# Two attentions side by side: the projections of the first one move into the loop of the second

## The chip, the cores and the metric

The kernel runs on one core of a Trainium2 chip. The metric is the device time of one execution in microseconds; the median of three runs before the change is 1738.47 us.

Names used below: PE is the matrix engine (TensorE), PEld its weight loads, DVE VectorE, ACT ScalarE, POOL GpSimd, SP the engine that issues most DMAs. PSUM has eight banks of 128 x 512 fp32 here, tile `ps_st`, numbered 0 to 7.

## The reference

Two attention blocks over 2048 positions and 640 features, 32 heads of 20 features each, with inputs of their own; the result is `[a, b]` along the features. Block A looks back over a dilated window, block B is full attention:

```python
qkv = (x @ wqkv).reshape(B, S, 3, H, Dh)          # both blocks, S = 2048, H = 32, Dh = 20
# A: 8 keys per query, at distances 0, 2, ... 14; keys before position 0 are masked
idx = pos[:, None] - (arange(8) * 2)[None, :]
logits = einsum("bhsd,bhswd->bhsw", q, kg) * Dh ** -0.5
a = einsum("bhsw,bhswd->bhsd", softmax(where(mask, logits, -1e9)), vg) @ wo
# B: all keys
p = softmax(einsum("bhqd,bhkd->bhqk", q, k) * Dh ** -0.5)
b = einsum("bhqk,bhkd->bhqd", p, v) @ wo
```

## The kernel before

Every projection is done in split precision: each operand is a rounded "hi" and the rest "lo", and three products hi·hi, hi·lo, lo·hi (`PASSES`) are summed. With five chunks of 128 features (`KC = 5`) one result tile takes 15 matmuls. ACT makes hi by a copy that rounds, DVE or POOL make lo by a subtraction.

**Ahead of the loop.** In this order: A's q and k (three sets of columns, 512, 256 and 512 wide, over 16 tiles of 128 rows), B's q and k (10 column blocks by 4 row blocks, 40 groups of 15 full matmuls with 512 columns), then the v of A and of B in blocks (`v_group`), between which PE computes score maxima for the first `LEAD = 52` steps. q, k, v go to DRAM and come back in the layout that the attention wants (`b_pieces`). A's attention runs on POOL, with help from DVE and ACT (`a_attention`), and begins while B's q and k are projected (`a_pace`).

**The loop** goes over B's attention. A unit is four heads (`g`) by 512 queries (`qc`), 32 units; a unit has 16 key blocks of 128; so there are `NS = 512` steps, a unit's key block each. A step needs

- four score halves: each is one matmul with 62 weight rows (three times 20 for the split, 2 for the maxima) and 512 columns, and one exp on ACT into an `e` tile. Two heads lie in the upper and two in the lower 64 rows of PE, so two halves run side by side;
- four maxima halves (60 rows) for the unit to come, each reduced by DVE from PSUM, singly or two banks at once;
- one value product: four matmuls of 32 output rows each, by heads (`b_pv`).

The order in which these pieces stand is written out in a string, `ORDER`, for the first 488 steps; the last `TAIL = 24` steps are regular. Its tokens: `Y` one score half and one maxima half side by side, `S` two score halves, `M` two maxima halves with one reduce over two banks, `N` two with two reduces, `V` a value product and the end of a step (here the product of two steps earlier, `LAG = 2`), `H` three of the 15 pairs of a group of A's output projection, `j` a small transpose. The digits are PSUM banks. PE executes exactly this order, as do ACT and DVE their own parts: each engine's queue is strictly in program order.

In `b_pv` two key blocks are summed in a bank. ACT copies the sum to SBUF (`more`), POOL adds it to the unit's sum (`braw`), eight times in a unit less one. At a unit's end the sums of exps are inverted by way of DRAM (`normalize`) and POOL multiplies.

POOL's share in each step is set by `begin(i)`: pieces of A's attention are issued as long as POOL's estimated time stays within `AHEAD` of `i * STEP`, `STEP = 2.36` us. A finished tile of A is transposed by DVE and DMA (`a_turn`, `turn_parts`), and projected by `H` tokens (`out_chunk`): two matmuls of 64 rows and 320 columns side by side, into two banks, whose two results ACT copies out and POOL adds.

B's output projection starts when a block of 512 queries has all its heads. The blocks are worked off with full 320-column groups between the last steps (`fill`), and the last block after the loop.

All engine instructions are recorded by one helper, so every row of the profile names line 71; rows are told apart by tiles and shapes.

Of the kernel before, what the change touches and what calls it, by code (L numbers as in the profile page):

```python
# [16 lines left out]
D = 640  # L17
# [12 lines left out]
PAD = WIN - 1  # L30
PASSES = ((0, 0), (0, 1), (1, 0))


# [6 lines left out]
PB = 6  # L40
NQC = 4
NKB = 16
NS = NG * NQC * NKB
LEAD = 52
TAIL = 24
R_AHEAD = 3
LAG = 2
NEG = -1.0e30
STEP = 2.36
AHEAD = 2.4  # L50
QK_US = 3.42
V_US = 2.72
A_SLOW = 0.91
A_FROM = 1
# [3 lines left out]

# [17 lines left out]
def attention_pair(ctx, tc, xa, wqk_a, wv_a, wo_a, xb, wqk_b, wv_b, wo_b, oa, ob):  # L76
    nc = tc.nc
    PS = bass.MemoryType.PSUM
    const = ctx.enter_context(tc.tile_pool(name="const", bufs=1))
    sb = ctx.enter_context(tc.tile_pool(name="sb", bufs=1))  # L80
    ps = ctx.enter_context(tc.tile_pool(name="ps", bufs=1, space=PS))
# [10 lines left out]
    loop = [None, False]  # L92

    def odd(n):

        return n if loop[0] is None else n + (now[0] + n - loop[0] + 1) % 2

    soft_jobs, turn_jobs = [], []
    at_once = [True]
# [6 lines left out]
    def job(jobs, n, fn, *args):  # L106

        jobs.append((now[0] + n, fn, args))
        if at_once[0]:
            run_jobs(jobs, 1)  # L110

    def tick():
        now[0] += 1
        for fn, args in due.pop(now[0], ()):
            fn(*args)


    psb = ps.tile([128, 8, 512], F32, name="ps_st")
    free = list(range(4))
    pair = [0]  # L120
    taken = {}
    given = []

    def bank():

        n = given.pop(0) if given else free.pop(0)
        t = psb[:, n]
        taken[id(t)] = (None if loop[0] is not None and loop[1] else n, t)
        return t

    def give(t):

        n = taken.pop(id(t))[0]
        if n is not None:
            free.append(n)

    def wide():

        pair[0] += 1
        return psb[:, 4 + 2 * (pair[0] % 2):6 + 2 * (pair[0] % 2)]  # L140

    def all_banks():
        while True:
            w = [wide(), wide()]
            for n in range(4):
                yield w[n % 2][:, n // 2]
                t = bank()
                give(t)
                yield t

# [10 lines left out]
    wait = [1]  # L161

    def split(hi, lo, src, tag="stg", second=None, first=None):

        t = sb.tile([128, 640 if tag == "stg" else 1024], F32, tag=tag, bufs=3 if tag == "stg" else PB, name="stg")
        raw = t[:, :src.free_size()] if len(src.shape) == 2 else (
            t[:, :src.shape[1] * src.shape[2]].rearrange("p (k c) -> p k c", c=src.shape[2]))
        sp.dma_start(raw, src)

        def parts():  # L170
            (first or act.copy)(hi, raw)
            (second or dve).tensor_tensor(lo, raw, hi.bitcast(F32), ALU.subtract)
        after(odd(wait[0]), parts)

    PAIRS = ((0, 2), (2, 4), (4, 5))

    def columns(n):

        return (sb.tile([128, 2, KC - 1, 512], F32R, tag="big", bufs=4, name="xn"),
                sb.tile([128, 2, 1, 512], F32R, tag=f"last{n % 4 // 2}", bufs=2, name="xl"))  # L180

    def chunk(t, xi, k):
        return t[k // (KC - 1)][:, xi, k % (KC - 1)]

    def x_pieces(x, n, second=None):

        t = columns(n)
        src = x[:, n * 512:(n + 1) * 512].rearrange("(k p) c -> p k c", p=128)

        def piece(a, b):  # L190
            u = t[a // (KC - 1)]
            m = a % (KC - 1)
            split(u[:, 0, m:m + b - a], u[:, 1, m:m + b - a], src[:, a:b], "p", second)
        return t, [lambda a=a, b=b: piece(a, b) for a, b in PAIRS]

    def wide_pieces(src, second=None, first=None):

        w = [sb.tile([128, KC, 320], F32R, tag="w", bufs=4, name="ww") for _ in range(2)]
        return w, [lambda a=a, b=b: split(
            w[0][:, a:b], w[1][:, a:b], src[:, a:b], second=second, first=first or second and gp.tensor_copy) for a, b in PAIRS]  # L200


    WA = 512
    A_COLS = [0, 512, 768, 2 * D]
    NA = len(A_COLS) - 1
    AK = ((0, 3), (3, KC))

    def a_parts(w, to, raw, k0, k1):
        for half, (a, b) in enumerate(AK):
            a0, b0 = max(a, k0), min(b, k1)  # L210
            if a0 < b0:
                u = slice(a0 - a, b0 - a)
                act.copy(w[0][half][:, u, to], raw[:, a0 - k0:b0 - k0])
                dve.tensor_tensor(w[1][half][:, u, to], raw[:, a0 - k0:b0 - k0], w[0][half][:, u, to].bitcast(F32), ALU.subtract)

    def a_piece(w, to, src, k0, k1, tag="stg"):

        n = to.stop - to.start
        t = sb.tile([128, 640], F32, tag=tag, bufs=3 if tag == "stg" else 2, name="stg")
        if src.shape[1] == k1 - k0:  # L220
            raw = t[:, :(k1 - k0) * n].rearrange("p (k c) -> p k c", c=n)
            sp.dma_start(raw, src)
        else:
            raw = t[:, :n].unsqueeze(1)
            sp.dma_start(t[:, :512].rearrange("p (m c) -> p m c", c=128), src)
        after(wait[0], a_parts, w, to, raw, k0, k1)

    def a_weight():
        return [[sb.tile([128, 3, WA], F32R, tag="w", bufs=4, name="wc"),
                 sb.tile([128, 2, WA], F32R, tag="akv", bufs=4, name="wd")] for _ in range(2)]  # L230

    def a_pieces(g):
        w, out = a_weight(), []
        c0, end = A_COLS[g:g + 2]
        c = c0
        while c < end:
            n = min(128 - c % 128, end - c)
            out.append(lambda to=slice(c - c0, c - c0 + n), src=wqk_a[c // 128][:, :, c % 128:c % 128 + n]:
                       a_piece(w, to, src, 0, KC))
            c += n  # L240
        return w, out

    def m_pieces(m):
        w = sb.tile([128, 2, KC, 128], F32R, tag="w", bufs=4, name="w")
        return w, [lambda: split(w[:, 0], w[:, 1], wqk_b[m])]

    def rows15(p, o, W):

        for k in range(KC):
            for i, (wi, xi) in enumerate(PASSES):  # L250
                pe.matmul(p[:, :320], o(xi, k), W[wi][:, k], start=(k == 0 and i == 0), stop=(k == KC - 1 and i == 2))

    def a_rows(p, x, t, g, W, ks, passes=PASSES):
        n = A_COLS[g + 1] - A_COLS[g]
        for k in ks:
            for wi, xi in passes:
                pe.matmul(p[:, :n], chunk(x, xi, k)[:, t % 4 * 128:t % 4 * 128 + 128], W[wi][k // 3][:, k % 3, :n],
                          start=(k == 0 and (wi, xi) == PASSES[0]), stop=(k == KC - 1 and (wi, xi) == PASSES[-1]))

    def a_store(p, g, t):  # L260

        c0, end = A_COLS[g:g + 2]
        r = sb.tile([128, WA], F32, tag="ao", bufs=3, name="ro")
        act.copy(r[:, :end - c0], p[:, :end - c0])
        hf, r0 = divmod(t * 128, HS)
        c = c0
        while c < end:
            m, c1 = divmod(c, D)
            n = min(D - c1, end - c)
            dst, pad = ((qa_d, 0), (ka_d, PAD))[m]  # L270
            after(1, sp.dma_start, dst[hf, pad + r0:pad + r0 + 128, c1:c1 + n], r[:, c - c0:c - c0 + n])
            c += n

    def store_rows(p, dst):
        r = sb.tile([128, 320], F32, tag="r", bufs=4, name="ro")
        act.copy(r, p[:, :320])
        if id(p) in taken:
            give(p)
        after(1, sp.dma_start, dst, r)


    NT = S // 128
    banks = all_banks()


    W = a_weight()
    XA = [columns(0)]
    for k in range(KC):
        a_piece(W, slice(0, WA), wqk_a[:4, :, k].rearrange("m p c -> p m c"),
                k, k + 1, ("stg", "stg", "stg", "vb", "vb")[k])  # L290
        split(chunk(XA[0], 0, k), chunk(XA[0], 1, k), xa[k * 128:(k + 1) * 128, :512], "p")
    tick()
    t, more = x_pieces(xa, 1)
    XA.append(t)
    for fn in more:
        fn()
    tick()
    wait[0] = 3
    loads = []
    for n in (2, 3):  # L300
        t, more = x_pieces(xa, n)
        XA.append(t)
        loads += more
    ident = sb.tile([128, 128], F32, tag="aot", bufs=1, name="ident")
# [3 lines left out]
    warm = bank()  # L308
    for _ in range(19):
        pe.transpose(warm[:, :128], ident, ident)  # L310
    give(warm)

    mask = const.tile([128, WIN, H], F32, name="mask")
    gp.memset(mask, 0.0)
# [891 lines left out]
```

## Time and profile before

| quantity | value |
|---|---|
| runs | 1738.47 us median (1737.33 to 1738.79) |
| span of the profiled execution | 1736.3 us |
| first value product starts | 458.47 us |
| value product of step 480 starts | 1604.87 us |
| last value product starts | 1687.64 us |
| PE busy | 1724.5 us (99%) |
| DVE busy | 1348.7 us (78%) |
| ACT busy | 1338.9 us (77%) |
| POOL busy | 1266.2 us (73%) |

The busy time of an instruction runs from its start to its end. Instructions of one engine overlap at their edges, so the distance from one start to the next is shorter than the mean duration. In a row of a timeline stand the start, the length, the engine, the operation, output <- inputs and the count; in brackets what it waited for and how long.

### The profile page before, as it was taken

How to read it: one execution, taken by the hardware profiler on the slowest of the kernel's cores; microseconds unless marked ns; L12 is line 12 of the kernel's file. 1: busy time of each engine (PE TensorE's matmuls, PEld its weight loads, DVE VectorE, ACT ScalarE, POOL GpSimd, SP SyncE). 2: the span in 40 equal slices, each digit the busy share in tenths (PEclk: the TensorE clock that was granted, in tenths of full speed). 3: DMA queues.
4: the chain of work that ended last, by engine and by line, in shares of the span. 5: the costliest groups of instructions: out<-in, count | busy, mean ns of one | idle time of the engine just before them, and what ended most of it. 6: DMA issues, size and time to landing. Idle time of an engine off the chain costs nothing.

```text
span 1736.3 us, 34687 instructions
## 1 busy us (share of the span) xinstructions
PE 1724.5 (99%) x12711; PEld 1006.0 (58%) x12711; DVE 1348.7 (78%) x1825; ACT 1338.9 (77%) x2658; POOL 1266.2 (73%) x1122
## 2 busy tenths in 40 slices
PE   9999999999999999999999999999999999999999
PEld 8988889999545544444344444444444455434569
DVE  3113223988799999999999999999999999999300
ACT  4323224232699999999999999999999999999981
POOL 0000950999899999999999999999999963544242
PEclk9999999999999999999999999999999999999999
DMA  6347878866754365345436434542643532111123
GB/s 227 119 139 239 304 261 273 259 204 187 199 151 125 96 161 153 93 136 158 135 95 173 126 119 127 170 135 88 158 143 106 147 95 61 46 36 53 33 76 113
DMA packets 194436, 248.29 MB, mean 143 GB/s; under 512 B 89309, under 2 KB 114397, under 8 KB 193273
## 3 DMA queue, kind: packets, MB, share of 16 engines
q1 hardware_dynamic: 193688, 245.41, 47.1%
q8 instruction: 100, 1.64, 0.4%
q14 instruction: 72, 0.58, 0.1%
q10 hardware_dynamic: 576, 0.66, 0.1%
HBM read 181.08 MB, written 64.91 MB: 142 GB/s over the span
## 4 chain that ended last, share of the span: by engine, by line
PE 90%; POOL 4%; DVE 2%; ACT 1%; DMA 1%; issue 1%; SPq 0%; POOLq 0%; ACTq 0%; DVEq 0%
PE ps_st L71 90%; POOL akv L71 2%; DVE mx L71 1%; ACT e L71 1%; POOL xn L71 1%; DMA stg<-wv_b 0%; SPq L71 0%; POOL ww L71 0%; POOL xl L71 0%; POOL ao L71 0%; ACT more L71 0%; DMA vb_d<-ve 0%; POOL al L71 0%; DMA s_d<-sm 0%; DMA rb<-s_d 0%
## 5 line engine op out<-in xcount | busy, mean ns | idle before, releaser
L71 DVE TENSOR_REDUCE mx<-ps_st 128x1 f32<-128x512 f32 (+1 forms) x1504 | 1227.6, 875 | 57.3 <-PE ps_st L71 47.8
L71 ACT ACTIVATE e<-ps_st 128x512 f32<-128x512 f32 x2048 | 1066.7, 627 | 30.7 <-PE ps_st L71 16.8
L71 PE MATMUL ps_st<-bk,bq 60*128 60x512 f32 x2048 | 553.4, 436 | 1.0 <-ACT ve L71 0.5
L71 PE MATMUL ps_st<-bq,bk 62*128 62x512 f32 x2048 | 548.7, 433 | 5.6 <-ACT ve L71 3.0
L71 PE MATMUL ps_st<-e,vb 128*32 128x512 f32 x4096 | 543.0, 604 | 0.4
L71 PEld LDWEIGHTS ps_st<-bq,bk 62*128 62x128 f32 x2048 | 274.8, 184 | 403.3 <-ACT e L71 246.5
L71 POOL TENSOR_TENSOR braw<-braw,more 128x512 f32<-128x512 f32 x224 | 288.2, 1287 | 85.5 <-ACT more L71 85.1
L71 PEld LDWEIGHTS ps_st<-bk,bq 60*128 60x128 f32 x2048 | 257.1, 184 | 108.7 <-DVE mx L71 61.2
L71 POOL TENSOR_TENSOR akv<-akv,aq 128x1280 f32<-128x1280 f32 x64 | 188.9, 2951 | 166.4 <-DVE w L71 166.3
L71 POOL TENSOR_TENSOR akv<-akv 128x640 f32<-128x640 f32 (+3 forms) x304 | 282.2, 928 | 14.4
L71 ACT COPY ro<-ps_st 128x320 f32<-128x320 f32 (+2 forms) x172 | 73.7, 463 | 171.1 <-PE ps_st L71 122.7
L71 PE MATMUL ps_st<-ww,xn 64*128 64x320 f32 (+1 forms) x1776 | 187.1, 309 | 0.0
L71 PEld LDWEIGHTS ps_st<-ww,xn 64*128 64x128 f32 (+1 forms) x1776 | 175.7, 186 | 14.6 <-ACT e L71 8.3
L71 PEld LDWEIGHTS ps_st<-e,vb 128*32 128x32 f32 x4096 | 82.1, 108 | 149.0 <-issue 75.4
L71 POOL TENSOR_TENSOR akv<-akv,al 128x1280 f32<-128x1280 f32 x64 | 151.6, 2368 | 0.2
L71 ACT COPY more<-ps_st 128x512 f32<-128x512 f32 x224 | 136.3, 609 | 3.5 <-PE ps_st L71 1.5
L71 PE MATMUL ps_st<-xn,w 128*128 128x512 f32 x480 | 115.8, 390 | 0.0
L71 PEld LDWEIGHTS ps_st<-xn,w 128*128 128x128 f32 x480 | 90.1, 188 | 19.3
L71 ACT CAST pr<-ps_st 128x512 fp32r<-128x512 f32 x40 | 23.5, 587 | 98.8 <-PE ps_st L71 96.0
L71 PE MATMUL ps_st<-ww,aot 64*128 64x320 f32 x960 | 99.7, 308 | 0.0
L71 DVE TENSOR_TENSOR pr<-ps_st,pr 128x512 fp32r<-128x512 f32 x40 | 27.6, 691 | 86.7 <-ACT pr L71 86.7
L71 PEld LDWEIGHTS ps_st<-ww,aot 64*128 64x128 f32 x960 | 90.3, 186 | 5.8 <-POOL ao L71 0.6
(65 smaller groups left out, 1062.5 us busy)
## 6 DMA issues: line engine op xcount, KB each, us to landing
akv<-ka_d SPq DMA_DIRECT2D x128, 320.0 KB
akv<-va_d SPq DMA_DIRECT2D x128, 320.0 KB
kb_d<-pr SPq DMA_DIRECT2D x20, 512.0 KB
qb_d<-pr SPq DMA_DIRECT2D x20, 512.0 KB
bk<-kb_d SPq DMA_DIRECT2D x16, 640.0 KB
bq<-qb_d SPq DMA_DIRECT2D x64, 160.0 KB
stg<-xb SPq DMA_DIRECT2D x16, 512.0 KB
rb<-s_d SPq DMA_DIRECT2D x128, 64.0 KB
```

What stands on the lines that cost most here:

```text
L71: return self.tc.keep_in_program_order(op(*a, **k))
```

## The change

Only B's q, k and v are projected ahead of the loop: the 40 groups of q and k as before, then 16 groups of v with the maxima of 32 steps between.

A's q, k and v become 48 small groups in the loop (12 sets of 320 columns, the second six sets for the second half of the rows, four groups a set). A group makes two tiles of 128 x 320. It has 30 `F` tokens, each two matmuls of 64 rows and 320 columns side by side, one for each result, and holds its two banks throughout; rows are exchanged after 15, so that both halves of the features end up in the same bank. The 16 groups of A's output projection and 12 of B's take the same form (the halves are no longer added by POOL). 70 of the 76 groups are in the `ORDER`, six are left for the end.

The products of all 16 key blocks of a unit are summed in one bank; ACT copies it once, to the single tile `misc`. `V` now computes its own step's product. The `e` tiles are seven of 512 x 2 columns (in tiles called `big` and `last`). A's attention on POOL starts when its rows are there, about step 80, with `STEP = 2.8`. At the end the last unit's sums are broadcast by a matmul with a selection matrix and inverted by DVE.

```diff
-LEAD = 52
-TAIL = 24
-LAG = 2
-STEP = 2.36
+LEAD = 32
+NP = 7
+STEP = 2.8
...
-        if part == 0:
-            accs[u] = bank()
-        acc = accs[u]
-        for j in range(GH):
-            pe.matmul(acc[32 * j:32 * j + 32, :], stacks[g][2][:, kb, j * VC:j * VC + 32], P[i][j % 2][:, j // 2],
-                      start=(part == 0), stop=(part == 1))
...
-            more = spare[n % 2][:, n // 2 % 2]
-            act.copy(more, acc)
-            after(2, pool, raws[u], raws[u], more, ALU.add)
+        if kb == 0:
+            accs[u] = psb[:, ns[0]]
+            acc_n[0] = ns[0]
+        acc = accs[u]
+        for j in range(GH):
+            pe.matmul(acc[32 * j:32 * j + 32, :], vs[u // NQC][:, kb, j * VC:j * VC + 32], P[i][j % 2][:, j // 2],
+                      start=(kb == 0), stop=(kb == NKB - 1))
+        del P[i]
+        if kb == NKB - 1:
+            raw = misc[:, :512]
+            act.copy(raw, accs.pop(u))
+            if u < NU - 1:
+                normalize(raw, u, (lambda: out_last(u % NQC, raw)) if u // NQC == NG - 1 else None)
...
+    def f_tokens(lhs, rhs, n, ns):
+        for second in range(2):
+            for k in range(KC):
+                for i, (wi, xi) in enumerate(PASSES):
+                    for r in range(2):
+                        w = r ^ second
+                        rows = slice(r * HALF, r * HALF + HALF)
+                        pe.matmul(psb[:, ns[w], :n], lhs(w, xi, k)[rows], rhs(wi, k)[rows],
+                                  start=(second == 0 and k == 0 and i == 0), stop=(second == 1 and k == KC - 1 and i == 2))
+                    yield
...
+            parts(AW[si][0][:, :, c:c + n], AW[si][1][:, :, c:c + n], raw, second=gp if si < 6 else dve, end=1)
...
+    def a_group(si, n, a, ns):
+        if n % 2 == 0 and a == 0:
+            if si + 1 < NA:
+                spaced(set_pieces(si + 1, 3), 1, 2)
+        x, W = XA[n], AW[si]
+        yield from f_tokens(lambda w, xi, k: chunk(x, xi, k)[:, (2 * a + w) * 128:(2 * a + w + 1) * 128],
+                            lambda wi, k: W[wi][:, k], 320, ns)
+        for w in range(2):
+            store_rows(ns[w], dst[hf, pad + r0:pad + r0 + 128, si % 2 * 320:si % 2 * 320 + 320])
+            if si % 6 in (3, 5):
+                after(3, a_rows.__setitem__, si % 6 // 5, t + 1)
...
-        "Y07S61M2Y45V0Y71S26M3Y05V7Y06M3S52Y71V0Y26M3S75VY71M5S24S03N17V2Y06S15Y34VM0S74Y56V3Y70S21N46VY70M4S12S63N07V1"
...
+        "Y10Y32M5S47S10M2V4Y75Y61S02Y37Y56VS10Y72Y36VY51Y20Y76VY35Y21F07FFFFY36FFY52FFFY13FFY56FFFY21VM5S32VY31Y56V"
...
+    pe.matmul(psb[:, acc_n[0]], ident, raw, start=True, stop=True)
+    dve.reciprocal(misc[:, 512:], psb[:, acc_n[0]])
+    dve.tensor_tensor(raw, raw, misc[:, 512:], ALU.mult)
+    out_rows(qc, raw, (sp, act))
...
```

The order on PE in the middle of the loop, before (`e` are the exps, `vb` the values, `bq` and `bk` B's queries and keys; a row counts equal instructions that follow each other; the two halves of a pair stand in one row or in two):

```order
L71 MATMUL ps_st<-bq,bk 128x512
L71 MATMUL ps_st<-bk,bq 128x512 x3
L71 MATMUL ps_st<-bq,bk 128x512 x2
L71 MATMUL ps_st<-e,vb 32x512 x4
L71 MATMUL ps_st<-bq,bk 128x512
L71 MATMUL ps_st<-bk,bq 128x512 x3
```

and in the changed kernel (queries and keys are `last` and `big` here, the weights of a projection `w`):

```order
L65 MATMUL ps_st<-big,vb 32x512 x4
L65 MATMUL ps_st<-last,big 128x512
L65 MATMUL ps_st<-big,last 128x512
L65 MATMUL ps_st<-last,big 128x512
L65 MATMUL ps_st<-big,last 128x512
L65 MATMUL ps_st<-w,big 128x320 x10
L65 MATMUL ps_st<-last,big 128x512
L65 MATMUL ps_st<-big,last 128x512
L65 MATMUL ps_st<-w,big 128x320 x4
L65 MATMUL ps_st<-last,big 128x512
L65 MATMUL ps_st<-big,last 128x512
L65 MATMUL ps_st<-w,big 128x320 x6
```

Between a score or maxima pair and the next now stand two to five `F` pairs (x4 to x10).

ACT in the loop, before:

```order
L71 ACTIVATE e<-ps_st 128x512 x7
L71 COPY more<-ps_st 128x512
L71 ACTIVATE e<-ps_st 128x512 x7
L71 COPY ro<-ps_st 128x320 x2
L71 ACTIVATE e<-ps_st 128x512 x4
L71 COPY more<-ps_st 128x512
```

and now:

```order
L65 ACTIVATE big<-ps_st 128x512 x3
L65 COPY ro<-ps_st 128x320 x2
L65 ACTIVATE big<-ps_st 128x512 x3
L65 COPY misc<-ps_st 128x512
L65 ACTIVATE big<-ps_st 128x512 x2
L65 ACTIVATE last<-ps_st 128x512
L65 CAST w<-stg 128x5x128
```

The copies of partial sums are gone; one copy a unit (`misc`) remains, and the roundings of A's weights (`CAST w`) have come in.

More of the change, by code (lines that the diff above doesn't have):

```diff
@@ L108, in job, with big, last, wtile @@
         jobs.append((now[0] + n, fn, args))
[L109 to L115, printed above, removed]
-    psb = ps.tile([128, 8, 512], F32, name="ps_st")
[L119 to L149, printed above, removed]
+    misc = const.tile([128, 1024], F32, name="misc")
+    psb = ps.tile([128, 8, 512], F32, name="ps_st")
+    def big(shape, dtype=F32R):
+        return sb.tile([128, *shape], dtype, tag="big", bufs=5, name="big")
+    def last(shape, dtype=F32R):
+        return sb.tile([128, *shape], dtype, tag="last", bufs=9, name="last")
+    def wtile(shape):
+        return sb.tile([128, *shape], F32R, tag="w", bufs=4, name="w")
+    def akv(shape, dtype=F32R):
+        return sb.tile([128, *shape], dtype, tag="akv", bufs=4, name="akv")
+    def columns():
+        return big((2, KC - 1, 512)), last((2, 512))
+    def chunk(t, xi, k):
+        if len(t) == KC:
+            return t[k][:, xi]
+        return t[0][:, xi, k] if k < KC - 1 else t[1][:, xi]
+    kst, qm, qs, pside = {}, {}, {}, []
+    def p_tile(t):
+        s = t % NP
+        if s > 3:
+            return last((2, 512), F32)
+        return pside[0][:, s * 1024:(s + 1) * 1024].rearrange("p (r c) -> p r c", r=2)
     qa_d = dr.tile([2, HS, D], F32, name="qa_d")
@@ L196, in wide_pieces @@
[L196 to L214, printed above, removed]
@@ L274, in store_rows @@
[L274 to L287, printed above, removed]
-    for k in range(KC):
-        a_piece(W, slice(0, WA), wqk_a[:4, :, k].rearrange("m p c -> p m c"),
-                k, k + 1, ("stg", "stg", "stg", "vb", "vb")[k])
-        split(chunk(XA[0], 0, k), chunk(XA[0], 1, k), xa[k * 128:(k + 1) * 128, :512], "p")
+    live = [0]
@@ L292, in attention_pair @@
     tick()
[L293 to L296, printed above, removed]
+    for k in range(KC):
+        xb_piece(1, k, 1)
     tick()
[L298 to L304, printed above, removed]
+    ident = const.tile([128, 128], F32, name="ident")
     gp.memset(ident, 0.0)
@@ new lines, in attention_pair, with out_matmuls @@
+    out_rows(qc, raw, (sp, act))
+    while due or bg or f_left:
+        tick()
+        run_bg(9)
+        leftover()
+    end = [psb[:, (acc_n[0] + 1 + n) % 8] for n in range(8)]
+    def out_matmuls(n, ks):
+        for k in ks:
+            for i, (wi, xi) in enumerate(PASSES):
+                pe.matmul(end[n][:, :320], chunk(OB[qc], xi, k)[:, n // 2 * 128:n // 2 * 128 + 128], WO[n % 2][wi][:, k],
+                          start=(k == 0 and i == 0), stop=(k == KC - 1 and i == 2))
+    for n in range(8):
+        out_matmuls(n, range(KC - 1))
```

1326 lines of the change are left out of this document (635 added, 691 removed).

## The prediction

> **What bounds the kernel now.** I read the page first: busy times, the slices, the chain that ended last.
>
> ```profile
> span 1736.3 us, 34687 instructions
> PE 1724.5 (99%) x12711; PEld 1006.0 (58%) x12711; DVE 1348.7 (78%) x1825; ACT 1338.9 (77%) x2658; POOL 1266.2 (73%) x1122
> PE 90%; POOL 4%; DVE 2%; ACT 1%; DMA 1%; issue 1%; SPq 0%; POOLq 0%; ACTq 0%; DVEq 0%
> ```
>
> PE is busy for 99% of the span, but matmuls overlap in these records, so I price PE's work by the distance from one start to the next. Then the view by windows, cut where the first and the last value product (the "V" of the order) of the loop's 480 first steps start, plus the last 31 steps and the tail; columns are length, then busy time (instructions) of PE, PEld, DVE, ACT, POOL, granted clock, DMA share, GB/s:
>
> ```profile
> 0.00:458.47 458.47, 453.67 (x3311) 398.62 (x3311) 211.36 (x230) 140.91 (x256) 222.27 (x200) 1.00 0.68 219
> 458.47:1604.87 1146.40, 1144.35 (x8524) 516.75 (x8522) 1116.89 (x1566) 1114.31 (x2233) 1005.86 (x888) 1.00 0.42 120
> 1604.87:1687.64 82.77, 81.33 (x572) 46.56 (x575) 16.84 (x25) 75.11 (x152) 27.84 (x26) 1.00 0.19 53
> 1687.64:1736.30 48.66, 45.16 (x312) 44.05 (x304) 3.60 (x7) 8.54 (x19) 10.21 (x11) 1.00 0.35 108
> ```
>
> Ahead of the loop PE alone is full; in the loop DVE and ACT each show 97% too. The unit prices come from PE's timeline:
>
> ```profile
> 120.08 2.21 PE L71 MATMUL ps_st<-wc,xn 128*128 128x512 f32 x9
> 123.53 2.21 PE L71 MATMUL ps_st<-wc,xn 128*128 128x512 f32 x9
> 345.10 1.94 PE L71 MATMUL ps_st<-ww,xn 64*128 64x320 f32 x24
> 347.32 0.69 PE L71 MATMUL ps_st<-bk,bq 60*128 60x512 f32 x4
> 537.34 1.07 PE L71 MATMUL ps_st<-e,vb 128*32 128x512 f32 x8
> 538.34 0.49 PE L71 MATMUL ps_st<-bk,bq 60*128 60x512 f32 x1
> 539.24 1.06 PE L71 MATMUL ps_st<-e,vb 128*32 128x512 f32 x8
> 541.24 0.39 PE L71 MATMUL ps_st<-bk,bq 60*128 60x512 f32 x1
> 541.48 0.68 PE L71 MATMUL ps_st<-ww,aot 64*128 64x320 f32 x6
> 541.92 0.39 PE L71 MATMUL ps_st<-bq,bk 62*128 62x512 f32 x1
> 1682.50 1.92 PE L71 MATMUL ps_st<-e,vb 128*32 128x512 f32 x16
> 1684.36 2.03 PE L71 MATMUL ps_st<-ww,xn 128*128 128x320 f32 x12
> 1695.30 1.92 PE L71 MATMUL ps_st<-ww,xn 128*128 128x320 f32 x12
> 1697.49 1.92 PE L71 MATMUL ps_st<-ww,xn 128*128 128x320 f32 x12
> ```
>
> 15 full 512-column matmuls lie between 120.08 and 123.53: 0.230 us each. 15 full 320-column ones between 1695.30 and 1697.49: 0.146. 30 half-height ones (24 and the 6 of the next record group) between 345.10 and 347.32, two side by side: 0.148 a pair, and three pairs between 541.48 and 541.92: 0.147. I call such a pair F. A pair of score or maxima halves (P) takes 541.48 - 541.24 = 0.24; I take 0.235, a mean over the loop. One V with three P lies between 537.34 and 539.24: 1.90 - 3 x 0.235 = 1.19. Two V in a row take 1.86 (1682.50 to 1684.36), so the first of two costs 0.88 when the second pays the exit.
>
> DVE and ACT are priced in the same way, from runs of instructions back to back:
>
> ```profile
> 899.79 1.84 DVE L71 TENSOR_REDUCE mx<-ps_st 128x1 f32<-128x512 f32 x3
> 901.90 1.82 DVE L71 TENSOR_REDUCE mx<-ps_st 128x2 f32<-128x1024 f32 x2
> 448.94 2.07 ACT L71 ACTIVATE e<-ps_st 128x512 f32<-128x512 f32 x4
> L71 ACT ACTIVATE e<-ps_st 128x512 f32<-128x512 f32 x1504 | 784.8, 629 | 22.9 <-PE ps_st L71 13.3 <-ACT e L71 0.3
> ```
>
> One exp lasts 0.63, four together 2.07: 0.48 from start to start. A maxima reduce comes to 0.60, a two-bank one (the second record group is one of each) to 1.13; a copy of 512 columns like an exp, 0.475. By these prices the loop's first 480 steps hold 1077 us of PE work, 94.0% of 1146.4, 1095 of DVE's and 1052 of ACT's. So three engines stand within 5%, and the loop pays for whichever is behind at the moment. The waits say the same:
>
> ```profile
> PEld ps_st L71 <- ACT e L71: 338.1, 547, 1.2
> PEld ps_st L71 <- DVE mx L71: 175.9, 360, 0.9
> ```
>
> PE's next weights wait for a bank that ACT, or else DVE, is still reading.
>
> **The change part by part.** *Ahead of the loop.* A's q, k, v leave it; 600 full 512-column matmuls (B's q and k), 480 F (B's v), 70 P of early maxima and 19 small ones stay: 600 x 0.230 + 480 x 0.147 + 70 x 0.235 + 4 = 229 us. The same count for the kernel before gives 449 against 458.5 measured. Part of those 9 us is one place:
>
> ```profile
> 447.65 0.43 ACT L71 COPY ve<-ps_st 128x320 f32<-128x320 f32 x1 [7.43 <-DMA vb_d<-ve]
> 448.13 0.50 PE L71 MATMUL ps_st<-bq,bk 62*128 62x512 f32 x1 [2.98 <-ACT ve L71]
> 449.77 2.61 PE L71 MATMUL ps_st<-ww,xn 128*128 128x320 f32 x9
> 440.00:460.00 20.00, 16.56 (x96) 12.89 (x98) 9.09 (x11) 7.93 (x17) 18.66 (x24) 0.91 0.75 199
> ```
>
> ACT waits 7.4 us for a buffer's store, PE then stands for 3 us, and the granted clock of these 20 us is 0.91. I charge such a gap 5 us with its slowed matmuls. The Trainium skill, "TensorE: Matmul & The Clock Gate", Part 1, says that an idle window of about 3.4 us throttles the clock by half; the drop behind this gap agrees. The new stage has five buffers for these stores, and I give it 6 us over its sum: **235** (bounds 231, nothing lost beyond the 1.4 us start, and 243, two such gaps). DVE (131 us of work) and ACT (56) are covered.
>
> *The loop's first 480 steps.* They take over the A projections and hold, by the new order: 1920 F (1260 pairs in the whole program before, 2580 now), 1924 P, 480 V of which 42 stand directly behind another. PE: 1920 x 0.147 + 1924 x 0.235 + 438 x 1.19 + 42 x 0.88 = 282 + 452 + 521 + 37 = **1292**. DVE gets the lo halves of the later weight sets, and, since fewer maxima stand ahead of the loop (LEAD 32 for 52) and single halves replace two-bank reduces, more reduces: 1452 x 0.598 + 234 x 1.131 + 73 of small things = 1206. ACT loses 224 copies of partial sums; POOL loses their adds:
>
> ```profile
> L71 ACT COPY more<-ps_st 128x512 f32<-128x512 f32 x224 | 136.3, 609 | 3.5 <-PE ps_st L71 1.5
> L71 POOL TENSOR_TENSOR braw<-braw,more 128x512 f32<-128x512 f32 x224 | 288.2, 1287 | 85.5 <-ACT more L71 85.1
> ```
>
> 224 x 0.475 = 106 us off ACT, 288 off POOL. ACT has 1928 exps x 0.477 + 30 unit sums x 0.475 + 128 copies of 320 columns x 0.31 (two a group) + 23 for halves of weights = 997; POOL, by the means of its groups, 888. Neither saving shortens PE's work. What they give is fewer waits in the loop: ACT falls from 92% of the stage to 74%.
>
> How much of its sum does a stage lose? Where the loop before already has many F, it loses little. Two stretches of 16 steps with 45 F each, the F alone and then all:
>
> ```profile
> 533.47:575.20 41.73, 9.22 (x90) 8.35 (x90) 2.27 (x2) 1.00 0.42 129
> 1412.00:1455.20 43.20, 9.27 (x90) 8.63 (x90) 4.55 (x4) 1.00 0.30 77
> 533.47:575.20 41.73, 41.72 (x350) 21.52 (x349) 40.34 (x58) 39.54 (x82) 40.63 (x40) 1.00 0.42 129
> ```
>
> The first holds 45 F, 65 P and 16 V: 6.6 + 15.3 + 19.0 = 40.9 of PE's work in 41.73, a share of 0.98. Taking stretch by stretch the larger of PE's and DVE's sum, the stretches with 30 F or more come to 199.3 us in 205.8, a share of 0.968; those without F, where DVE leads, to 0.92. Why: an F needs no new bank for half a group (30 F write two banks), so PE works on while ACT and DVE empty the others. In the changed order nearly every 16 steps have 45 to 90 F. The larger of PE and DVE, stretch by stretch, is 1292 + 22 (nine stretches where DVE leads) = 1314. Divided by 0.968: **1357**. Bounds: PE's share 0.98 gives 1318, today's 0.94 gives 1374.
>
> A rule speaks against it. The Trainium skill, "TensorEngine Tiling (Array Packing)", Key Properties, says that a change of tiling mode drains TensorE. V agrees: 1.19 alone, 0.88 behind another. F between P does not: three F and one P from 541.24 to 541.92 take 0.68, and 3 x 0.147 + 0.235 = 0.68. So I charge nothing for the some 1,600 changes between F and P in the new order.
>
> *Sums of a unit in one bank.* V's 16 products of a unit now keep a bank for the whole unit, and an F group two for 30 F. Five banks are left for P. The copy at a unit's end waits until the tile `misc` has been stored, four steps (some 11 us) after that store is issued; behind it on ACT stand the exps, and for these PE. The trace of before has no such wait. From below 0 (the store has landed), from above the 7.43 us of the row above for a store that is late: 29 units x a few tenths if seldom late. I take 0 and keep 8 for the range.
>
> *The last 31 steps and the tail.* 180 F, 60 P, 32 V (18 directly behind another): 26.5 + 14.1 + 16.7 + 15.8 = 73; the stage before stood 5 us over its sum of 78, so **76**. From the last V on, 180 + 120 full 320-column matmuls stand before and after: 43.8 of the 48.66 us. The new broadcast by PE, the reciprocal of 128x512 (below 0.24 us, the row of 16 columns, it can't be; 32 times that, 7.7, is its upper end) and the scaling run beside 26 us of leftover groups, which hide them; without that cover they cost up to 9. I take **49**.
>
> ```profile
> L71 DVE RECIPROCAL sm<-sm 128x16 f32<-128x16 f32 x23 | 5.6, 242 | 0.0
> ```
>
> Sum: 235 + 1357 + 76 + 49 = 1717 us of span, against 458.5 + 1146.4 + 82.8 + 48.7 = 1736.3 now. The median of the runs, 1738.5, lies 2.2 above the span. Forecast: **1719 us**, 1.1% faster.
>
> **The rivals.** *The share stays at 0.94.* The loop before shows it as a whole, though not where F are frequent: 235 + 1374 + 76 + 49 + 2 = 1736, no change.
>
> *F fills every gap.* 0.98 as in the stretch at 533: 1680.
>
> *Late data, slower.* PE works strictly in order, and an F group whose columns or weights are not in stops everything behind it, P and V too. The weights of a set now come by DMA, ACT and POOL (which also runs A's attention, later than before) only one set of four groups ahead. POOL's sum between steps 145 and 416 is 733 us beside 748 of the leading engine, so it has hardly any slack, and A's output groups wait for POOL. Before, POOL's lateness showed little on PE, since only 48 groups hung on it. With 5 us a gap, five gaps eat 24 us and cancel the gain; eight or ten give some 1755.
>
> *Too few banks, slower.* With five banks instead of six to eight, a bank's round (matmul 0.40, exp 0.62, both by the durations shown, plus handover) must fit within about 1.2 us between its uses. It decides where handovers exceed 0.2 us. If 800 of the tokens that stand between F each wait 0.1 us: +80, some 1800. For it: the two waits quoted above are already of this kind. Against: F fall between, 0.147 each. The Trainium skill, "TensorEngine Tiling (Array Packing)", Gotcha 1, warns that row tiling raises the pressure on PSUM.
>
> *Every change between F and P drains.* 1,600 x 0.10 = +160, some 1880; only V shows it.
>
> **How the numbers follow.** Forecast 0.50, its own range 1692 to 1740 (1314 by 0.985 or 0.955, and 4 us for the other terms); share 0.94: 0.13; F fills: 0.12; late data 0.13; banks 0.10; drains 0.02. A measurement of this kernel tells about 0.2% (3.5 us) from no change. Faster: 0.48 + 0.12 + 0.06 of the second = 0.66; same: 0.02 + 0.06 + 0.01 of late data = 0.09; slower, the rest: 0.25. The range runs from 1672 to 1764: it leaves out banks, drains and the far end of the others.
>
> **What would show it.** First V at 231 to 243 us. From there to step 480 1318 to 1375 us with PE's waits for ACT well under today's 338 us. If late data: idle before F's weights of over 1 us released by POOL, DMA or ACT `w`, and slices with a clock below 1.00. If banks: PEld waits for `big`/`last` (the exps' outputs) as large as today or larger. If drains: three F and a P over 0.75 us. Wrong outright: a loop whose 480 steps need over 1400 us, or a stage ahead of the loop over 250.

## The result: 1.6% slower, and where the time went

The changed kernel takes 1766.74 us (median of 4, 1765.02 to 1768.46) against 1738.63 before: a ratio of 1.016, interval 1.0145 to 1.0174. The forecast was 1719 us, with a range from 1672 to 1764.

The page of the changed kernel begins (rows as in the prediction's first fence):

```profile
span 1764.0 us, 37708 instructions
PE 1716.7 (97%) x14273; PEld 1028.8 (58%) x14273; DVE 1394.8 (79%) x2083; ACT 1239.4 (70%) x2415; POOL 957.2 (54%) x857
PE 81%; DVE 9%; DMA 3%; POOL 3%; ACT 2%; issue 2%; SPq 1%; DVEq 0%; POOLq 0%; ACTq 0%
```

ACT and POOL have lost 100 and 309 us of work as the diff says. PE now holds 81% of the chain that ended last, not 90%, and DVE has 9% of it, where it had 2%. The view by windows, cut at the first V, at steps 128, 336 and 480, at the last V and at the end:

```profile
0.00:234.18 234.18, 230.92 (x1720) 202.31 (x1720) 132.60 (x148) 66.83 (x123) 20.46 (x29) 1.00 0.64 204
234.18:603.80 369.62, 369.50 (x3296) 212.35 (x3295) 323.41 (x487) 300.44 (x585) 103.01 (x106) 1.00 0.34 97
603.80:1248.30 644.50, 611.30 (x5199) 338.14 (x5198) 573.37 (x888) 485.54 (x946) 570.81 (x491) 0.98 0.61 177
1248.30:1641.88 393.58, 386.10 (x3031) 186.19 (x3033) 358.19 (x555) 312.81 (x609) 235.55 (x203) 0.99 0.46 128
1641.88:1714.69 72.81, 72.81 (x733) 45.27 (x729) 0.54 (x3) 65.69 (x137) 27.39 (x30) 1.00 0.27 78
1714.69:1764.00 49.31, 46.10 (x314) 44.52 (x306) 6.71 (x7) 8.07 (x19) 0.00 (x0) 1.00 0.22 77
```

The stage ahead of the loop gives back 458.5 - 234.2 = 224.3 us, the last 31 steps 10.0, and the tail takes 0.6 more. The first 480 steps need 1407.7 us instead of 1146.4: 261.3 more, of which some 214 are PE work moved in (1291 of work by the prediction's prices, against 1077). The other 47 are new loss, waiting and matmuls at a lowered clock, and the windows say where. (By the clock records of this trace the granted clock stands at 0.50 for 37.5 us of this stage, in seven places, so the lowered clock accounts for at most 19 us.) For single stretches I have again priced what the order issues there with the prediction's prices. Steps 0 to 128 hold 360.2 us of PE work in 369.6, a share of 0.975. Steps 128 to 336 hold 577 us of the leading engine's work (PE or DVE, 16 steps at a time) in 644.5, with PE idle for 33 us and the granted clock at 0.98: 68 us over the sum.

What stands in that stretch is seen in the timeline around 1018 us (start, length, engine, operation; in brackets the idle time before it and what ended that; `...` stands for rows left out):

```profile
1013.81 2.33 POOL L65 TENSOR_TENSOR akv<-akv 128x320 f32<-128x320 f32 x3
...
1014.62 0.81 DVE L65 TENSOR_TENSOR w<-stg,w 128x640 fp32r<-128x640 f32 x1
...
1016.50 2.93 POOL L65 TENSOR_TENSOR akv<-akv,aq 128x1280 f32<-128x1280 f32 x1
...
1017.33 2.78 DVE L65 TENSOR_TENSOR w<-stg,w 128x640 fp32r<-128x640 f32 x1
...
1019.51 2.00 POOL L65 TENSOR_TENSOR akv<-akv 128x640 f32<-128x640 f32 x1
...
1020.77 0.50 PE L65 MATMUL ps_st<-big,last 60*128 60x512 f32 x1 [2.00 <-DVE mx L65]
```

The same subtraction, the lo half of a piece of A's weights, takes 0.81 us at 1014.62, where POOL's instruction of that moment had 0.06 us left, and 2.78 at 1017.33. The second began while POOL was in a multiplication that started at 16.50 and ended at 19.43; it ended 0.7 us after that. DVE's maxima reduces stand behind it in the queue, the banks they read stay taken, and PE stands for 2 us.

This is the pattern of the whole loop. Three more rows, the first two beside each other, the third where POOL was idle:

```profile
621.61 1.54 POOL L65 TENSOR_TENSOR ao<-akv 128x640 f32<-128x640 f32 x1
621.73 2.10 DVE L65 TENSOR_TENSOR w<-stg,w 128x640 fp32r<-128x640 f32 x1 [1.56 <-ACT w L65]
...
1568.94 0.82 DVE L65 TENSOR_TENSOR w<-stg,w 128x640 fp32r<-128x640 f32 x1
```

The loop has 20 subtractions of 640 columns. Eleven began while a POOL instruction had 0.69 us or more to run; every one of them ended 0.68 or 0.69 us after that instruction, and they took 1.37 to 2.78 us. The other nine began with POOL idle or within the last 0.12 us of its instruction, and took 0.81 to 0.83. The Trainium skill, "SBUF — State Buffer", Who interferes with whom, says that a DVE instruction with two SBUF inputs contends with a GpSimd instruction that reads SBUF, through a port pair that is locked exclusively, while a reduce does not contend. The rows above and the runs below agree with both halves. This rule stood against the change, and the prediction did not weigh it.

### The profile page after: what moved, and what is told of

Its sections match the earlier page's. It is cut to its first block, busy times and chain, and to the rows that moved or that the text cites. A ratio compares the mean times of both kernels' runs of the same rounds, so it can differ in the third digit from the quotient of the medians.

```text
span 1764.0 us, 37708 instructions
## 1 busy us (share of the span) xinstructions
PE 1716.7 (97%) x14273; PEld 1028.8 (58%) x14273; DVE 1394.8 (79%) x2083; ACT 1239.4 (70%) x2415; POOL 957.2 (54%) x857
## 4 chain that ended last, share of the span: by engine, by line
PE 81%; DVE 9%; DMA 3%; POOL 3%; ACT 2%; issue 2%; SPq 1%; DVEq 0%; POOLq 0%; ACTq 0%
PE ps_st L65 81%; DVE mx L65 7%; DVE w L65 2%; POOL akv L65 2%; ACT big L65 1%; ACT last L65 1%; SPq L65 1%; DMA s_d<-sm 0%; DMA last<-qb_d 0%; POOL ao L65 0%; DMA stg<-xa 0%; DMA last<-xb 0%; DMA stg<-wo_a 0%; DMA ot_b<-misc 0%; POOL misc L65 0%
## 5 line engine op out<-in xcount | busy, mean ns | idle before, releaser
L65 ACT ACTIVATE big<-ps_st 128x512 f32<-128x512 f32 x1172 | 636.4, 619 | 162.5 <-PE ps_st L65 149.2
L65 PE MATMUL ps_st<-big,last 60*128 60x512 f32 x2048 | 694.6, 434 | 10.9 <-DVE mx L65 9.9
L65 PE MATMUL ps_st<-last,big 62*128 62x512 f32 x2048 | 671.8, 427 | 28.3 <-DVE mx L65 15.5
L65 ACT ACTIVATE last<-ps_st 128x512 f32<-128x512 f32 x876 | 475.1, 619 | 117.6 <-PE ps_st L65 108.4
L65 PEld LDWEIGHTS ps_st<-last,big 62*128 62x128 f32 x2048 | 315.8, 186 | 396.1 <-DVE mx L65 121.9
L65 PE MATMUL ps_st<-w,big 64*128 64x320 f32 (+1 forms) x4560 | 491.7, 308 | 2.3 <-DVE mx L65 2.3
L65 PEld LDWEIGHTS ps_st<-w,big 64*128 64x128 f32 (+1 forms) x4560 | 432.4, 187 | 33.0 <-DVE mx L65 5.3
L65 PE MATMUL ps_st<-big,vb 128*32 128x512 f32 x2344 | 387.2, 609 | 0.0
L65 PEld LDWEIGHTS ps_st<-big,last 60*128 60x128 f32 x2048 | 311.2, 185 | 96.7 <-DVE mx L65 46.6
L65 PE MATMUL ps_st<-last,vb 128*32 128x512 f32 x1752 | 311.6, 611 | 0.1
```

What stands on the lines that cost most here:

```text
L65: return self.tc.keep_in_program_order(op(*a, **k))
```

## The experiments

All times are medians; the kernel before took 1739.0 to 1739.7 us beside these runs. "After" is the changed kernel with 1766.7. The code is shortened: `hi` and `lo` stand for slices of `AW[si]`, and `...` for lines left out. Windows and gaps are those of one profiled execution of each kernel.

**The subtractions left out.** For sets 6 to 11:

```diff
-            parts(hi, lo, raw, second=gp if si < 6 else dve, end=1)
+            if si < 6: parts(hi, lo, raw, second=gp, end=1)
+            else: act.copy(hi, raw)            # AW[si][1] = AW[si][0]
```

> Left out: the lo halves of A's weight sets 6 to 11 (18 subtractions on DVE); their matmuls read hi twice, in the same number, so the output differs. Theory 1 (these subtractions, drawn out by POOL, stand between DVE's maxima reduces, the banks come free late and PE waits): steps 128 to 288 fall from 489.9 us to 465 to 472, the whole to 1742 to 1750. Theory 2 (PE waits there because banks are too few or POOL's part of A's attention is late): steps 128 to 288 stay above 484, the whole above 1760.

Measured: 1751.5 us, 15.2 below after (ratio to before 1.0071, 1.0056 to 1.0086). Steps 128 to 288 went from 489.9 to 478.4 us, less than theory 1 alone said: gaps that have nothing to do with these subtractions stayed (4.6 us at step 189, 2.9 at step 159).

**A reduce in their place.**

```diff
+            else:
+                act.copy(hi, raw)
+                dve.tensor_reduce(scr, hi, AX.X, ALU.max)
```

> As the run with the 18 subtractions left out, but in place of each DVE reduces the hi piece of the same 640 or 320 columns (one operand in SBUF, same wait for ACT); output differs. If POOL's draw-out is the harm (theory 1a): each takes about 0.8 us whatever POOL does, the whole lies within 5 us above the run without them. If DVE's own time is the harm (theory 1b): the whole comes back to within 5 us of the changed kernel, 1762 to 1767.

Measured: 1756.4 us (1750.5 to 1759.0), 4.9 above the run without and 10.3 below after. The drawing-out counts for some 10 of the 15 us or more. The 4.9 us between the two runs are no more than the scatter of this one, and in the profiled executions they do not lie where the edit does. Steps 128 to 288 in after, in the run without the subtractions and in this one:

```profile
603.80:1093.70 489.90, 468.30 (x4063) 263.88 (x4062) 439.04 (x687) 377.15 (x736) 430.06 (x371) 0.99 0.61 180
```

```profile
604.10:1082.50 478.40, 464.61 (x4063) 265.69 (x4062) 418.02 (x669) 376.00 (x736) 423.11 (x371) 0.99 0.62 184
```

```profile
605.60:1084.50 478.90, 466.95 (x4067) 264.63 (x4068) 427.58 (x687) 376.52 (x736) 423.08 (x371) 0.99 0.62 184
```

Here 18 reduces, with the same wait for ACT as the subtractions, cost 0.5 us, and the subtractions 11.5. What this run took longer lies mostly in steps 288 to 320 (108.5 us instead of 105.5), where both kernels do the same. Between 604 and 1140 us of after, of the run with the reduce, and of the run with POOL's work cut down (below), and then ahead of the loop in the kernel before, the groups on DVE are:

```profile
L65 DVE TENSOR_TENSOR w<-stg,w 128x640 fp32r<-128x640 f32 x14 | 20.7, 1488 | 4.8 <-ACT w L65 4.6
```

```profile
L65 DVE TENSOR_REDUCE scr<-w 128x5 f32<-128x640 f32 x12 | 9.7, 812 | 4.9 <-ACT w L65 4.8
```

```profile
L65 DVE TENSOR_TENSOR w<-stg,w 128x640 fp32r<-128x640 f32 x16 | 15.9, 1000 | 4.8 <-ACT w L65 4.6
```

```profile
L71 DVE TENSOR_TENSOR ww<-stg,ww 128x640 fp32r<-128x640 f32 x4 | 3.2, 824 | 3.8 <-ACT ww L71 3.8
```

(Busy us, then the mean in ns.) 1488 ns beside a busy POOL, 1000 with POOL's instructions cut short, 812 for a reduce with one operand in SBUF beside a POOL as busy as in after; ahead of the loop the kernel before needed 824 for the subtraction. (The 14 and the 16 include a few pieces of A's output weights.)

**B's output weights split by ACT and POOL.**

```diff
-                spaced(wide_pieces(wo_b, WO, 0, 3, dve.tensor_copy) + wide_pieces(wo_b, WO, 1, 3, dve.tensor_copy), 1, 2)
+                spaced(wide_pieces(wo_b, WO, 0, 3, None, gp) + wide_pieces(wo_b, WO, 1, 3, None, gp), 1, 2)
```

> Only the hi and lo halves of B's output weights, 12 DVE instructions in steps 440 to 465, move to ACT (hi) and POOL (lo), which is nearly idle there. Theory 1: steps 448 to 464 fall from 48.5 us to 38 to 41, the whole by 7 to 10 us to 1757 to 1760. Theory 2 (banks): no change, since DVE's other work and the order stay, 1765 to 1768.

Measured: 1760.1 us (1755.5 to 1763.4), 6.6 below. Steps 448 to 464, after and in this run:

```profile
1558.90:1607.40 48.50, 45.18 (x256) 15.82 (x254) 43.16 (x65) 34.66 (x68) 9.59 (x11) 0.89 0.27 80
```

```profile
1561.10:1601.70 40.60, 39.67 (x258) 14.92 (x258) 36.88 (x52) 36.67 (x74) 16.94 (x17) 1.00 0.31 95
```

7.9 us of a stretch with 33.8 us of PE work, and POOL was nearly idle: here it was DVE's time alone, 6.3 us less of it, and the clock, back at 1.00 from 0.89.

**Sets 6 to 11 loaded ready-made.**

```diff
+                for x in range(2):              # sets 0 to 5, when split
+                    after(6 + 2 * x, sp.dma_start, aw_d[si, x], AW[si][x])
...
+        def reload(x):                          # sets 6 to 11
+            if x == 0: AW[si] = [wtile((KC, 320)) for _ in range(2)]
+            sp.dma_start(AW[si][x], aw_d[si - 6, x])
```

> Sets 6 to 11 are not split again: sets 0 to 5 store their hi and lo halves to DRAM and sets 6 to 11 load them ready-made (18 hi on ACT, 18 lo on DVE gone; about 10 MB more stored and 5 MB more loaded). Theory 1: as the run with the subtractions left out or a little below, 1738 to 1750. If the DMA queues there are the limit (theory 3, late data): gaps of over 1 us in front of F rows whose weights come late, and the whole stays above 1760.

Measured: 1746.7 us (ratio to before 1.004), 20.0 below after. This also takes the 18 roundings off ACT, so the 20 us are not the subtractions' price alone; leaving only these out gave 15.2. Steps 128 to 288, columns as above:

```profile
604.00:1075.20 471.20, 459.50 (x4063) 262.30 (x4062) 416.20 (x669) 367.67 (x719) 424.40 (x372) 0.99 0.65 198
```

489.9 before this edit. Some 15 MB more moved by DMA (272.4 instead of 257.7) cost nothing that shows.

**ACT's copies put back.**

```diff
         act.activation(P[i][pl][:, r], p, AF.Exp, scale=SCALE)
+        if pl and r and i % 2 and i % NKB > 1:
+            act.copy(P[i][0][:, 0], P[i][0][:, 0])
```

> Added to the changed kernel: 224 copies of 512 columns on ACT (an e tile onto itself, where before the partial sums were copied), some 106 us of ACT's time put back; nothing else. If ACT's relief is what the change lives on: 20 us or more slower, 1787 to 1810, with PE's waits for ACT growing. If PE and DVE lead in the changed order and ACT's relief was worth little: 0 to 10 us slower, 1766 to 1777.

Measured: 1800.9 us, 34.1 above after. The loop's first 480 steps, after and here:

```profile
234.18:1641.88 1407.70, 1366.89 (x11519) 736.68 (x11521) 1254.96 (x1927) 1098.79 (x2139) 909.38 (x798) 0.99 0.50 142
```

```profile
234.14:1670.09 1435.95, 1393.90 (x11519) 747.00 (x11521) 1260.41 (x1927) 1188.74 (x2349) 909.05 (x799) 0.99 0.48 140
```

28 us in the loop, spread over all of it (1 to 2 us in most stretches of 16 steps), and the rest behind step 480. That is 0.15 us for each copy, on an engine that is busy for 78% of the loop in after. It is not the price of the old copies, though. An old copy read a bank; a new one rewrites an `e` tile that the V of its step reads, so V waits for it too. The idle time before V's weight loads grew from 174.6 to 186.6 us, and the part of it that ends with ACT's `e` tiles from 4.2 to 38.2. So some 12 of the 28 us may come from this order of copy and V and not from ACT's time, and 34 us is an upper end of what taking the copies out was worth. Without those 12 there remain some 22, still more than the forecast gain of the whole change, 19.5.

**What comes late, mended.** Two more steps for x pieces, maxima rows loaded at once, tiles turned two steps later:

```diff
-            after(3, split_piece, k, raw)
+            after(5, split_piece, k, raw)
-        bg.extend([lambda r=r: one(r) for r in range(2)])
+        for r in range(2): one(r)
-            job(turn_jobs, 1 + k, part, k)
+            job(turn_jobs, 3 + k, part, k)
```

> Only things that come late are mended: the pieces of A's x get two more steps between load and split, the maxima rows are loaded at once and not behind other background work in the line, A's finished tile is turned two steps later. Theory 3 (late data): the gaps at steps 159, 189 and 334 (3.2, 4.8 and 4.7 us, with a slow clock behind them) go, the whole falls by 10 to 16 us to 1751 to 1757. Rival (they only move on to the next late thing, or POOL's pieces move with them): less than 4 us.

Measured: 1764.0 us (1756.5 to 1767.0), 2.8 below. The gaps at steps 159, 189 and 334 did go (steps 176 to 192: 41.0 us, 48.1 in after), but steps 400 to 416 took 55.1 instead of 49.3, with PE waiting there for A's tiles, and gaps at DVE's splits grew. The rival was right: a mend alone only moves on to the next late thing.

**Both output weights off DVE.** As for B's, and the same edit for A's.

> Both output weights are split by ACT (hi) and POOL (lo) and no more by DVE (24 instructions). Theory 1: steps 288 to 320 fall from 104.6 us by 8 to 12, steps 448 to 464 by 8 as before, the whole to 1746 to 1754. Rival (POOL, 90% busy at steps 288 to 320, comes late with A's attention in their place): steps 288 to 416 no shorter in sum than 291 us, the whole near 1760.

Measured: 1757.3 us (1751.4 to 1759.0), 9.5 below, in between. Steps 288 to 320 fell from 104.6 to 97.9 and steps 448 to 464 to 40.6, but steps 368 to 384 and 400 to 416 lost 9 us: in the first DVE waits 4.11 us for POOL's `ao` and PE 3.67 behind it, in the second PE waits for `big` from POOL. (The profiled execution was the fastest of the four.)

**All of these together** (A's and B's output weights split by ACT and POOL, sets 6 to 11 ready-made, and what comes late mended, with tiles turned one step later).

> The ready-made weight sets, the split of the output weights by ACT and POOL, and the three things that came late (the tile turned one step later, not two), all together; same result as the reference asks for. Theory 1 and 3 add up: 1766 less 20, 12 to 16 and 10 to 16, 1714 to 1726, below the kernel before, and PE's share of steps 0 to 480 at 0.955 or above, as forecast. Theory 2 (banks): no lower than 1740.

Measured: 1734.3 us (ratio to before 0.997, 0.9959 to 0.9981): faster than before, but above what was expected. Steps 400 to 416 took 62.1 us. PE's timeline there:

```profile
1440.96 0.41 PE L65 MATMUL ps_st<-w,big 64*128 64x320 f32 x2 [3.53 <-POOL big L65]
1442.57 0.63 PE L65 MATMUL ps_st<-w,big 64*128 64x320 f32 x2 [1.20 <-POOL big L65]
```

A's output groups wait at step 415 for a tile from POOL. POOL had the splits of A's output weights earlier, in steps 285 to 307, and the tiles are turned a step later than in after. With the later turn kept and the splits gone (the next run) the stretch takes 54 us, so 8 of the 13 us are the splits.

**All weights ready-made.** The output weights are split in steps 4 to 70, while POOL is idle, stored, and loaded like the sets; the sets and what comes late are as in the run before:

```diff
+    spaced([p for n, w in enumerate((wo_a[0], wo_a[1], wo_b[0], wo_b[1])) for p in wo_pieces(w, n)], 4, 5)
-                spaced(wide_pieces(wo_a, WO, 0, 3, dve.tensor_copy), 1, 2)
+                spaced(wo_load(0, 0), 1, 2)     # two loads; the other halves and wo_b likewise
```

> No weight is split in the loop after step 145: sets 6 to 11 come ready-made as before, and both output weights are split in steps 4 to 70, where POOL is idle, stored, and loaded ready-made; with the mends for late x pieces, maxima rows and (one step) turned tiles. Theory 1 and 3: the stretch of steps 400 to 416, 62.1 us with the splits on POOL, is back near 49, steps 272 to 288 near 42, the whole 1710 to 1722. Rival (POOL's part of A's attention is late by itself, with no splits on it): above 1728.

Measured: 1726.3 us (5 runs, 1722.5 to 1727.6), ratio to before 0.9929 (0.9915 to 0.9942): 40.5 below after, 0.7% faster than the kernel before. The loop's 480 steps:

```profile
233.95:1597.73 1363.78, 1350.42 (x11518) 733.30 (x11520) 1213.98 (x1885) 1093.46 (x2133) 916.20 (x810) 1.00 0.56 167
```

1363.8 us, where 1357 was forecast for the changed kernel; this execution was the fastest of the five, 3.8 us below their median. The gain is all in steps 128 to 336: 597.4 us instead of 644.5. The clock stands at 0.50 for 6.8 us of the loop, 37.5 in after. What is left over is mostly steps 400 to 416 (54 us, A's last tiles) and one wait of ACT's copy into `misc` for the store before (3.4 us of PE at step 352).

**A unit's sums go through earlier.** Every unit takes the shorter steps that the last four units had:

```diff
-        t = (1, 2, 5, 6, 7, 9, 10) if then else (1, 2, 7, 8, 9, 11, 12)
+        t = (1, 2, 5, 6, 7, 9, 10)
```

> As the run with all weights ready-made, and a unit's inverted sums go through two to three steps earlier, so that the one tile of sums is stored earlier and ACT's copy of the next unit does not wait for it. If those waits (1.6 us of PE at step 272 in the run before) matter: 3 to 8 us below it. If the order of POOL only moves: within 3 us.

Measured: 1735.0 us, 8.7 above; neither expectation held. In its trace DVE waits 4.67 us for POOL (`am`, a small step of A's softmax) at 647 us and PE 4.6 us behind it, a gap that was 1.1 before. The stretches around it, steps 96 to 144, are 8.5 us longer (151.2 against 142.7). I read it as POOL's pieces having moved against DVE's; it wasn't tested further.

**POOL's work cut down.** A's attention with a quarter of the columns in most of POOL's instructions, no order changed:

```diff
-    pool = gp.tensor_tensor
+    def pool(out, a, b, op):        # n: the columns, a quarter of them where wide
...
+        gp.tensor_tensor(cut(out), cut(a), cut(b), op)
```

> Left out: three quarters of the columns of most of POOL's instructions on A's attention (output differs); the changed kernel's order on every engine stays. If POOL is what draws DVE's splits out and what A's tiles wait for (theory 1a and 3): the 22 stretched subtractions come down to about 0.8 us, the gap at step 189 goes, the whole falls to 1735 to 1748. If POOL is not involved: above 1760.

Measured: 1738.7 us, 28.0 below after. The subtractions came down to a mean of 1000 ns, not quite to 0.8, and the gap at step 189 went. With POOL short and DVE's splits still in place, the changed kernel is level with the one before. A shorter POOL draws the splits out less and is also less late itself; this run does not part the two.

**DVE's reduces cut in half.**

```diff
-            dve.tensor_reduce(m4[:, :, pq, 2 * ch + j], psb[:, ns:ns + 2], AX.X, ALU.max)
+            dve.tensor_reduce(m4[:, :, pq, 2 * ch + j], psb[:, ns:ns + 2, :256], AX.X, ALU.max)
```

> DVE's maxima reduces read 256 of the 512 columns of a bank (the maxima only shift the exponent), some 0.27 us less each; nothing else changes. If DVE, with its splits in between, holds the banks that PE waits for (theory 1): the splits fit into DVE's free time, steps 128 to 480 fall by 40 us or more, the whole to 1700 to 1725. If ACT's and POOL's lateness hold PE (theory 3): less than 15 us, above 1750.

Measured: 1743.2 us (1734.9 to 1749.6), 23.5 below: between the two. A DVE with much free time still leaves the gaps at steps 159, 189, 306 and 334 (2.7, 4.4, 4.1 and 5.7 us in the profiled execution, the fastest of the ten), which are waits for a DMA, for POOL, for a run of drawn-out splits, and one (step 334) that the profile puts down to nothing. Theory 1 alone does not cover the loss; theory 1 and 3 together do.

## Why the prediction was wrong, point by point

- **Ahead of the loop**, 235 us: 234.2. **The last 31 steps**, 76: 72.8. **The tail**, 49: 49.3; its reciprocal took 3.36 us, hidden beside the leftover groups as said.
- **The loop's first 480 steps**, 1357 us: 1407.7. The step that failed is "the larger of PE and DVE, stretch by stretch, divided by 0.968". Its PE sum was right (1291), and so was the share where only what was costed happened: 0.975 in steps 0 to 128, and with all weights ready-made the whole loop took 1363.8. What the step had wrong is that the weight splits stand in DVE's sum at a fixed price ("73 of small things"; they lasted 101.8 us, 44.0 of these the 42 split instructions, which at the lengths they have beside an idle POOL come to some 26). Those that start while POOL is in A's attention last until POOL's instruction has ended, in a queue in which most other instructions free a bank for PE. So PE loses more than DVE's sum shows: the 18 subtractions cost 11.5 us of steps 128 to 288, reduces of 0.8 us in their place 0.5. The price in the whole: 15.2 us for these subtractions, 20.0 with ACT's roundings of the same sets, 6.6 for B's output weights, whose run of 12 instructions beside an idle POOL is DVE's plain time; all splits out and three late things mended, 40.5.
- **The share of 0.968** rested in part on a comparison of two measures. The five stretches with many F were taken by the larger of PE and DVE; the 0.92 of those without F is PE's own share (166 of 180 us). By the larger of the two, DVE's 175, they come to 0.97 as well. So the trace of before did not show that F shorten the waiting; that the share nearly held with the splits gone does not show it either.
- **Late data**, given 0.13 and 1745 to 1760 us, was the nearest rival, in sign and almost in size, but by another path. In the changed kernel itself, the F groups waited for weights or columns in none of the gaps quoted; only where POOL had more to do or the tiles were turned later did A's output groups wait for POOL, the path that the prediction had named. In the changed kernel it was DVE and ACT that waited, for POOL (step 189) or a DMA (step 159), with PE's banks behind them. "5 us a gap" was about right where the clock fell with it: steps 176 to 192 took 7 us less without the 4.7 us gap.
- **Too few banks** was not what cost the 47 us: the loop runs at its forecast pace with the same banks once the splits are gone. But added copies on ACT cost time in most of the loop, not all of it before V, which fits that how soon a bank is emptied sets part of the pace; that is not shown, and a bank more wasn't tried.
- **ACT's relief**, "fewer waits": right in kind, and its size, at most 34 us, was never worked out as a term of the sum. Without it the change would have come to as much as 1801 us.
- **Draining between F and P**: not seen, as forecast. Steps 0 to 128, with 615 F, stay within 2.6% of the sum.
- **The single tile `misc`**, 0 to 8 us: within that range in the changed kernel, where ACT waited some 9 us in all at that copy and PE less; 3.4 us of PE once with the splits gone.

## What to carry to other kernels

An engine's work in a loop is not only a sum to set against its free time. A small instruction put into the queue that frees the buffers of the critical engine is cheap while it stays small and that engine's queue has room (18 reduces cost 0.5 us here, but 12 splits where DVE led cost 7.9), and it costs far more once another engine can draw it out. Before such work is moved into a loop, see which other engine holds what it needs: here a DVE subtraction with both operands in SBUF beside POOL work went from 0.82 to 1.49 us in the mean, and up to 2.78. And what is computed twice in a loop for want of space (the weight halves) may be stored and loaded, if DMA has room.

## What the runs showed of the hardware that was not expected

The granted clock fell after gaps shorter than the one on which I had built my 5 us, and not after others that were longer. PE's waits in the changed kernel around 1572 us, and one-microsecond windows of the same place:

```profile
1571.55 0.50 PE L65 MATMUL ps_st<-last,big 62*128 62x512 f32 x1 [0.64 <-DVE mx L65]
1574.01 0.79 PE L65 MATMUL ps_st<-big,last 60*128 60x512 f32 x1 [0.42 <-DVE mx L65]
```

```profile
1571.00:1572.00 1.00, 0.45 (x2) 0.19 (x2) 1.00 (x2) 0.60 (x2) 0.00 (x0) 1.00 0.66 193
1572.00:1573.00 1.00, 0.91 (x7) 0.50 (x5) 0.97 (x3) 0.85 (x2) 0.19 (x1) 0.90 0.12 45
1573.00:1574.00 1.00, 0.59 (x1) 0.08 (x1) 1.00 (x3) 1.00 (x3) 0.92 (x2) 0.50 0.00 0
...
1578.00:1579.00 1.00, 1.00 (x6) 0.20 (x8) 1.00 (x2) 1.00 (x3) 0.00 (x0) 0.50 0.66 170
1579.00:1580.00 1.00, 1.00 (x10) 0.14 (x4) 0.97 (x3) 0.48 (x1) 0.00 (x0) 0.69 0.55 170
1580.00:1581.00 1.00, 0.83 (x6) 0.34 (x6) 0.61 (x2) 0.61 (x2) 0.00 (x0) 1.00 0.46 119
```

The clock (third number from the end) stands at half for about 6.8 us, from 1572.8 on, although the longest that PE had stood in the seven microseconds before was 0.64 us at a stretch. After the 3.1 us gap at 691 us it stayed at 1.00 throughout. So the length of a single gap does not decide. The Trainium skill, "TensorE: Matmul & The Clock Gate", Part 1, describes an activity window that runs on its own time, about 3.4 us long; two such windows are 6.8 us, which fits, but which windows count as idle can't be read from these rows. Over the changed kernel the mean granted clock is 0.989; with all weights ready-made it is 0.998.
